# A fused attention and feed-forward kernel: group 0's second product by seven block products, w_out cast by its load, one block product added in PSUM

## The chip, the cores and the metric

The kernel runs on one core of a Trainium2 chip. The time is device microseconds of one execution, and two kernels are compared by it. The core has five engines that the text names as the profile does: PE (the matrix engine; PEld is its loading of weights, which runs beside the matmuls), DVE, ACT, POOL (GpSimd) and SP, whose queue issues most DMAs. All DMAs run on the core's 16 DMA engines.

## The reference

```python
def phi(x, c, s):                       # c, s: cosine and sine of the position
    r = np.maximum(x, 0.0)
    return np.concatenate([r * c, r * s], axis=-1)
q_p, k_p = phi(q, cos_w, sin_w), phi(k, cos_w, sin_w)
kv = np.einsum('bhsf,bhsd->bhfd', k_p, v)
z = np.sum(k_p, axis=2)
num = np.einsum('bhsf,bhfd->bhsd', q_p, kv)
den = np.einsum('bhsf,bhf->bhs', q_p, z)[..., None] + 1e-06
x = (num / den).transpose(0, 2, 1, 3).reshape(B * S, H * D)
h = x @ w_in
out = np.maximum(0.01 * h, h) @ w_out
```

Eight batches of 576 tokens with eight heads of 64 give 4608 rows of 512; `w_in` is 512 x 2048 and `w_out` 2048 x 512. Inputs and output are float32.

## The kernel before

The rows are worked off in nine groups of 512. Groups 0 to 7 are the first 512 tokens of a batch each, group 8 holds the last 64 tokens of all eight. For a group, q is masked and scaled into fp16 (`q_part`), as is k (`k_part`), and v is cast (`v_main`, with `v_tail` or `v_mask` for the last 64 tokens). PE then makes kv of the batch (`kv_sums` in two halves for batches 0 and 1, `kv_all`, line 290, later), and numerator and denominator (`num`, line 381). DVE divides (line 397), and the result is transposed to `xT` by PE or by a DMA.

Group 0's first product runs as 128x512 matmuls (line 496), 16 column tiles m of `w_in` with four chunks each, and its second product too: `ffn2_mm` (line 629) adds 16 matmuls for each of four row tiles tt into a PSUM bank `ps_o`, 64 in all. Group 1's first product is plain as well. From group 2's first product and group 1's second on, each product is cut into 2x2 blocks and made by seven block products in place of eight (Winograd's form): `p1` (line 745) for the first product, `p2` (line 846) for the second, each matmul 128x256, with sums of blocks made by DVE (`x_sums`, `w1_sums`, `g_sums`, `w2_sums`). Some blocks of later groups are cut once more (`p4th`, line 963, 128x128).

One unit of `p1` covers four column tiles and has four PSUM banks: two that units take in turn (here called a), `SEED` and `JOIN`. Product 1 goes into a, and ACT copies it to `SEED` (`seed`, line 755), where product 2 is added and ACT takes the leaky ReLU of the sum (block 11, `lrelu`, line 758). Product 6 is added in a, copied by ACT to SBUF (`u_copy`, line 765); product 7 is added in a and copied too; product 4 is added, and ACT makes block 21. Product 5 goes into `JOIN`. DVE adds it to the second copy (`u_add`, line 252), product 3 is added in `JOIN`, DVE adds that to the first copy, and one activation over both copies makes blocks 12 and 22 (`u_lrelu`, line 772).

Loads are issued on SP's queue, in the order q, k and v of batch 0, `w_in` (eight DMAs of 512 KB), two of the four MB of `w_out`, q of batch 1, the third MB, halves of k and v of batch 1, the fourth MB, and so on. `w_in` and `w_out` come as float32 into staging tiles; POOL, DVE and ACT cast them into the fp16 tiles (`cast_w1`, `cast_w2`, line 249). The order of everything is written out by hand: each step is given a position, the table `PLACE` overrides positions, `OTHER` names steps that change between DVE and ACT, and the steps are issued in order of their positions. Each engine runs its part strictly in that order.

```python
    for _, _, f, args in sorted(line, key=lambda e: e[:2]):
        f(*args)
```

Of the kernel before, what the change touches and what calls it, by code (L numbers as in the profile page):

```python
# [18 lines left out]
def kernel(  # L19
# [429 lines left out]


# [172 lines left out]

    def ffn2_mm(g, i):
        tt, part = divmod(i, 4)
        if part == 0 and ("ps_o", g, tt) not in st:
            st["ps_o", g, tt] = psum("o", [P, DM], dt.float32, "ps_o")
        for m in range(4 * part, 4 * part + 4):
            nc.tensor.matmul(  # L629
                st["ps_o", g, tt],  # L630
                lhsT=st["g", g][:, m, tt * P : (tt + 1) * P],
                rhs=w2[:, m, :],
                start=(m == 0),
                stop=(m == NFT - 1),
            )
# [1167 lines left out]
```

## Time and profile before

| | us |
|---|---|
| median of three runs | 268.2 (266.79 to 268.61) |
| the profiled execution | 267.86 |
| its span, first to last instruction | 266.1 |
| first matmul of any kind, on blanks | 1.09 |
| group 0's first product has PE to itself from | 18.90 |
| group 0's second product begins | 31.01 |

The span is 1.8 us shorter than the execution's own time. Two views carry the reading: the table of windows, which gives each engine's busy time and the DMA engines' share in a stretch, and the chain of waits, which lists in order of time what the end was waiting for. A row of the timeline names in brackets how long the engine stood idle before it and what ended that.

### The profile page before, as it was taken

To read this page: it belongs to the slowest core of one execution; us is meant where nothing else is said; L and a number is where in the kernel's file an instruction comes from. 1 tells how busy PE (TensorE), PEld (TensorE's weight loads), DVE (VectorE), ACT (ScalarE), POOL (GpSimd) and SP (SyncE) were. 2 spreads that over 40 slices of the span, in tenths; PEclk is the share of its full clock that TensorE was granted. 3 is DMA by queue.
4 is the path that set the end of the run, shared out by engine and by line. 5 is a ranking of instruction groups with operands and counts; after the bars stand their busy time and mean duration, and the time that the engine had idled before them with its cause. 6 is when DMAs were issued, how large, how long until landed. Compare 5 with 4: busy or idle time off the path is not lost.

```text
span 266.1 us, 7209 instructions
## 1 busy us (share of the span) xinstructions
PE 260.3 (98%) x2874; PEld 229.7 (86%) x2874; DVE 233.5 (88%) x550; ACT 217.6 (82%) x400; POOL 9.9 (4%) x21
## 2 busy tenths in 40 slices
PE   8999999999999999999999999999999999999994
PEld 6885466765999889999999999999999999999994
DVE  5882799997998899999989899999999988996993
ACT  8756567876999999999889889999988877878751
POOL 1056001000000000000000000000000000000000
PEclk9999999999999999999999999999999999999999
DMA  6999999999999999998997899957645043300216
GB/s 222 357 395 410 401 388 370 370 213 303 273 242 145 278 312 210 332 146 264 265 229 181 248 288 235 141 200 170 92 101 197 22 80 60 121 1 4 98 65 155
DMA packets 87153, 57.09 MB, mean 215 GB/s; under 512 B 56656, under 2 KB 82256, under 8 KB 86608
## 3 DMA queue, kind: packets, MB, share of 16 engines
q1 hardware_dynamic: 86672, 56.24, 81.4%
q8 instruction: 22, 0.36, 0.6%
q10 hardware_dynamic: 448, 0.39, 0.5%
q14 instruction: 11, 0.09, 0.1%
HBM read 36.70 MB, written 9.44 MB: 173 GB/s over the span
## 4 chain that ended last, share of the span: by engine, by line
PE 89%; DMA 4%; DVE 2%; SPq 2%; ACT 1%; issue 0%; ACTq 0%
PE ps_h L745 30%; PE ps_o L846 24%; PE ps_h L496 10%; PE ps_o L963 8%; PE ps_o L629 5%; PE ps_num L381 3%; PE ps_kv L290 2%; DMA xT<-xs 2%; DMA vtl<-in_v_dram 2%; PE ps_h L846 2%; PE ps_h L963 1%; PE ps_numh L581 1%; PE ps_kvh L290 1%; SPq L93 1%; SPq L103 1%; DVE u L252 1%
## 5 line engine op out<-in xcount | busy, mean ns | idle before, releaser
L745 PE MATMUL ps_h<-xT,w 128*128 128x256 f16 x336 | 49.2, 273 | 0.2 <-DMA xT<-xs 0.2
L745 PEld LDWEIGHTS <-w 128*128 128x128 f16 x448 | 47.3, 113 | 1.0 <-issue 0.4
L846 PEld LDWEIGHTS <-g 128*128 128x128 f16 x408 | 38.7, 98 | 3.6
L252 DVE TENSOR_TENSOR u<-ps_h,u 128x512 f32<-128x512 f32 x56 | 38.4, 685 | 3.8 <-PE ps_h L745 2.5
L745 PEld LDWEIGHTS <-wa 128*128 128x128 f16 x336 | 35.9, 113 | 1.3 <-issue 1.0
L765 ACT COPY u<-ps_h 128x512 f32<-128x512 f32 x56 | 32.9, 592 | 4.3 <-PE ps_h L745 3.6
L758 ACT ACTIVATE g<-ps_h 128x512 f16<-128x512 f32 x56 | 33.8, 605 | 2.5 <-PE ps_h L745 2.3
L745 PE MATMUL ps_h<-xw,wa 128*128 128x256 f16 x224 | 33.6, 272 | 0.5 <-DVE u L252 0.3
L772 ACT ACTIVATE g<-u 128x1024 f16<-128x1024 f32 x28 | 29.7, 1065 | 2.3 <-DVE u L252 2.2
L496 PE MATMUL ps_h<-xT,w 128*128 128x512 f16 (+1 forms) x152 | 29.6, 345 | 0.0
L846 PEld LDWEIGHTS <-gs 128*128 128x128 f16 x256 | 24.4, 98 | 2.3
L846 PE MATMUL ps_o<-w,g 128*128 128x256 f16 x192 | 25.9, 273 | 0.0
L846 PE MATMUL ps_o<-wb,g 128*128 128x256 f16 x184 | 25.6, 272 | 0.0
L496 PEld LDWEIGHTS <-w 128*128 128x128 f16 x152 | 16.3, 113 | 9.0
L864 ACT COPY ob<-ps_o 128x512 f32<-128x512 f32 (+1 forms) x32 | 18.1, 566 | 2.9 <-PE ps_o L846 1.8
L397 DVE TENSOR_TENSOR xs<-ps_num,rden 128x512 f16<-128x512 f32 x28 | 19.4, 691 | 1.0
L846 PE MATMUL ps_o<-w,gs 128*128 128x256 f16 x120 | 17.0, 273 | 0.0
L755 ACT COPY ps_h<-ps_h 128x512 f32<-128x512 f32 x28 | 16.4, 584 | 0.7 <-PE ps_h L745 0.2
L745 PE MATMUL ps_h<-xT,wa 128*128 128x256 f16 x112 | 16.8, 273 | 0.0
L745 PE MATMUL ps_h<-xw,w 128*128 128x256 f16 x112 | 16.8, 273 | 0.0
L846 PE MATMUL ps_o<-wb,gs 128*128 128x256 f16 x120 | 15.9, 272 | 0.0
L629 PE MATMUL ps_o<-w,g 128*128 128x512 f16 x64 | 15.3, 379 | 0.0
(148 smaller groups left out, 502.0 us busy)
## 6 DMA issues: line engine op xcount, KB each, us to landing
qst<-in_q_dram SPq DMA_DIRECT2D x7, 1024.0 KB, 7.3
out_dram<-ob SPq DMA_DIRECT2D x14, 512.0 KB, 3.0
kst<-in_k_dram SPq DMA_DIRECT2D x6, 1024.0 KB, 8.6
vst<-in_v_dram SPq DMA_DIRECT2D x6, 1024.0 KB, 7.7
w1st<-in_moe_w_in_dram SPq DMA_DIRECT2D x8, 512.0 KB, 9.0
w2st<-in_moe_w_out_dram SPq DMA_DIRECT2D x4, 1024.0 KB, 12.4
kst<-in_k_dram SPq DMA_DIRECT2D x4, 512.0 KB, 7.1
vst<-in_v_dram SPq DMA_DIRECT2D x4, 512.0 KB, 6.4
```

The lines of the kernel that those rows point to most:

```text
L252: nc.vector.tensor_tensor(out=o, in0=a, in1=b, op=ALU.add)
L397: nc.vector.tensor_tensor(out=xs, in0=ps[:, :, 0 : 4 * NE].rearrange("p a (b e) -> p a b e", e=NE)[:, :, :, 0:D], in1=rden.rearrange("p (a ...
L496: nc.tensor.matmul(ps[:, lo:hi], lhsT=w1[m // 4][c // 2][:, c % 2, m % 4 : 512 : 4], rhs=st["xT", g][:, c, lo:hi], start=(c == 0 and lo == 0),
L629: nc.tensor.matmul(st["ps_o", g, tt], lhsT=st["g", g][:, m, tt * P : (tt + 1) * P], rhs=w2[:, m, :], start=(m == 0), stop=(m == NFT - 1),)
L745: nc.tensor.matmul(bank[:, p], lhsT=w(c), rhs=st["xb", g][n][:, c], start=(fresh and p == 0 and c == 0), stop=(c == 1), skip_group_check=True,
L755: nc.scalar.copy(bank1[bj], bank1[bi])
L758: nc.scalar.activation(st["g" + nm, g][:, 2 * t : 2 * t + 2], bank1[bi], AF.Lrelu)
L765: nc.scalar.copy(st["u", g, t][:, n], bank1[bi])
L772: nc.scalar.activation(st["gt", g][:, :, 1, 2 * t : 2 * t + 2], st["u", g, t], AF.Lrelu)
L846: nc.tensor.matmul(bank[..., lo:hi], lhsT=st[G2[n], g][:, m, pair * P : (pair + 1) * P], rhs=W2[n](m)[:, lo:hi], start=(fresh and m == 0), ...
L864: nc.scalar.copy(o_at(g, half_, col, pair), bank_of(bi, pair, pair is None))
L963: nc.tensor.matmul(quad_at(g, bi, *QUAD[i]), lhsT=lhsT, rhs=rhs, start=(m == 0 and (i == 2 or (i == 4 and g == NG - 1))), stop=(m == 3), s ...
```

## The change

Six things change.

1. Group 0's second product is made by seven block products: `ffn2_mm` goes, and `p2` is called for group 0 with 16 matmuls for each product. DVE makes the four sums of blocks of group 0's activations in halves (`g_sums`), all sums of `w_out` blocks are needed earlier (`w2_sums`), and the output leaves by four ACT copies, three DVE adds and two stores of 512 KB where it was four copies and four stores of 256 KB. A third PSUM bank (`third_bank`) holds products 5 and 3.
2. `load_w2` is issued by POOL straight into the fp16 tile `w2`, so that the DMA casts. `cast_w2` and its staging tiles go.
3. In a unit of `p1`, product 5 is copied to SBUF by ACT (`p5_copy`), DVE adds it to bank a and writes the sum into `SEED` (after products 1 and 6) and, after product 7, into `JOIN` (`p5_add`); product 3 is added in `SEED` by PE. Blocks 12 and 22 are then activated each from its bank. `u_copy`, `u_add`, `u_lrelu` go.
4. Group 1's first product, as plain as before, is issued in halves of a column tile (`f1_unit`).
5. Pools with several buffers take them in a fixed turn (`Turns`); the staging tiles by a list (`STAGE`).
6. `PLACE` and `OTHER` are other tables: nearly every step has another position, and `OTHER` names 96 steps, most of them maskings of q and k, where it named 25.

```diff
+    class Turns:
+        def tile(self, shape, dtype, name, tag=None, bufs=None):
+            tag, bufs = tag or name, bufs or self.bufs
+            n = self.count[tag] = self.count.get(tag, -1) + 1
+            n = self.order[n] if self.order else n % bufs
+            return self.places.tile(shape, dtype, name=name, tag=f"{tag}__{n}", bufs=1)
...
     def load_w2(i):
-        t = staged([P, 4, DM], "w2st", i > 1)
-        nc.sync.dma_start(t, w2v[i])
-        st["w2", i] = t
+        nc.gpsimd.dma_start(w2[:, 4 * i : 4 * i + 4, :], w2v[i])
...
-    def u_copy(g, t, n, bi):
-        if n == 0:
-            st["u", g, t] = tpool.tile([P, 2, 2, N2], dt.float32, name="u", tag="u")
-        nc.scalar.copy(st["u", g, t][:, n], bank1[bi])
-
-    def u_add(g, t, n, bi):
-        u = st["u", g, t][:, n]
-        add(u, bank1[bi], u)
+    def p5_copy(g, t, bi):
+        st["p5", g, t] = tpool.tile([P, 2, N2], dt.float32, name="p5", tag="p5")
+        nc.scalar.copy(st["p5", g, t], bank1[bi])
+
+    def p5_add(g, t, bi, to):
+        add(bank1[to], bank1[bi], st["p5", g, t])
...
+            banks = {2: SEED, 3: SEED, 5: JOIN}
...
+                (1, seed, (t, a, SEED)), (2, lrelu, ("11", t, SEED)),
+                (5, p5_copy, (t, JOIN)), (5.01, p5_add, (t, a, SEED)),
+                (7, p5_add, (t, a, JOIN)), (3, lrelu_12, (t, SEED)),
+                (7.01, lrelu_22, (t, JOIN)), (4, lrelu, ("21", t, a)),
...
+    def first_p2(n, bi, fresh):
+        for u in range(2):
+            for pair in range(2):
+                now(p2, 0, n, pair, u, bi, fresh and u == 0 and pair == 0)
...
         "first_loads": {
-            (0,): -940.5, (1,): -893.5, (10,): -869.33, (12,): -861.25
+            (0,): -999.8, (3,): -987.43, (2,): -876.5, (4,): -874.0, (1,): -856.83, (5,): -846.6,
```

How the change moves instructions is seen in three places. The first is POOL's queue at the program's start, up to the last step that POOL does at all; `vmain` is the cast v, `w_0_0` to `w_3_1` are the eight fp16 tiles of `w_in`. Before:

```order
L249 CAST vmain<-vst 128x8x64 x2
L249 CAST w_0_0_102<-w1st 128x512 x2
L249 CAST w_0_1_103<-w1st 128x512 x2
L249 CAST w_2_0_106<-w1st 128x1024
L249 CAST w_2_1_107<-w1st 128x1024
L249 CAST w_3_1_109<-w1st 128x1024
L249 CAST w_3_0_108<-w1st 128x1024
L249 CAST vmain<-vst 128x16x64
```

The same place now, where `w_113` is the fp16 tile of `w_out`:

```order
L162 DMA w_113<-in_moe_w_out_dram 128x2048
L266 CAST vmain<-vst 128x8x64 x2
L266 CAST w_0_0_105<-w1st 128x512
L162 DMA w_113<-in_moe_w_out_dram 128x2048
L266 CAST w_0_0_105<-w1st 128x512
L266 CAST w_0_1_106<-w1st 128x512 x2
L266 CAST w_2_1_110<-w1st 128x1024
L266 CAST w_2_0_109<-w1st 128x1024
L266 CAST w_3_0_111<-w1st 128x1024
L266 CAST w_3_1_112<-w1st 128x1024
L162 DMA w_113<-in_moe_w_out_dram 128x2048 x2
```

The first MB of `w_out` (its rows for m 0 to 3) now stands ahead of everything that POOL waits for, the third MB (m 8 to 11) between two casts of `w_in`, and the second and fourth behind the last of them.

The second place is DVE while PE does the end of group 0's first product. Before, with `w_110` the fp16 tile of `w_out`, `wa` sums of `w_in` blocks:

```order
L252 TENSOR_TENSOR wa_0_211<-w_2_0_106,w_2_1_107 128x1024
L255 TENSOR_TENSOR wa_0_213<-wa_0_211,w_0_0_102 128x1024
L249 CAST w_110<-w2st 128x2048
L252 TENSOR_TENSOR wa_1_212<-w_3_0_108,w_3_1_109 128x256x2
L255 TENSOR_TENSOR wa_1_214<-wa_1_212,w_1_0_104 128x256x2
L249 CAST w_110<-w2st 128x2048
L255 TENSOR_TENSOR wa_1_216<-w_1_1_105,wa_1_214 128x256x2
L241 TENSOR_SCALAR qp<-qst,cos_t 128x8x64
```

Now, with `gs` and `g` sums of group 0's activation blocks and `wb` sums of `w_out` blocks:

```order
L269 TENSOR_TENSOR wa_0_214<-w_2_0_109,w_2_1_110 128x1024
L272 TENSOR_TENSOR gs_518<-g 128x1024
L272 TENSOR_TENSOR wa_0_216<-wa_0_214,w_0_0_105 128x1024
L272 TENSOR_TENSOR gs_518<-g 128x1024
L272 TENSOR_TENSOR wb_220<-w_113 128x1024
L272 TENSOR_TENSOR w_113<-w_113 128x4x256
L272 TENSOR_TENSOR wb_221<-w_113,wb_220 128x1024
L272 TENSOR_TENSOR gs_519<-g,gs_518 128x1024
L269 TENSOR_TENSOR g<-g 128x4x256
L272 TENSOR_TENSOR wb_222<-w_113,wb_221 128x1024
```

The casts of `w_out` are gone, and the sums that the block products need stand in their place.

The third place is ACT in group 2's first product. Before, `ps_h_1221` and `ps_h_1222` are the banks a, `ps_h_1223` is `SEED` (`JOIN`, `ps_h_1224`, is read by DVE alone):

```order
L765 COPY u<-ps_h_1222 128x512
L755 COPY ps_h_1223<-ps_h_1221 128x512
L772 ACTIVATE g<-u 128x2x512
L758 ACTIVATE g<-ps_h_1222 128x512
L247 CAST vmain<-vst 128x16x64
L758 ACTIVATE g<-ps_h_1223 128x512
L765 COPY u<-ps_h_1221 128x512
```

Now `ps_h_1289` and `ps_h_1290` are the banks a, `ps_h_1291` is `SEED` and `ps_h_1292` is `JOIN`:

```order
L765 COPY p_1487<-ps_h_1292 128x512
L239 ACTIVATE vtail<-vtl,odd 128x4x64 x2
L759 ACTIVATE g<-ps_h_1289 128x512
L857 COPY ob<-ps_o_539 128x2x256
L264 CAST vmain<-vst 128x16x64
L759 ACTIVATE g<-ps_h_1291 128x512
L756 COPY ps_h_1291<-ps_h_1289 128x512
L759 ACTIVATE g<-ps_h_1292 128x512
```

The last activation that reads `SEED` in one unit now stands right ahead of the copy that fills `SEED` for the next; before, `SEED` was free after block 11, early in its unit.

More of the change, by code (lines that the diff above doesn't have):

```diff
@@ L60 @@
     const = pool("const", 1)
-    stage = pool("stage", 3)
+    stage = pool("stage", 3, order=STAGE)
     kvtail = pool("kvtail", 3)
@@ L68 @@
     xtpool = pool("xT", 2)
+    xwpool = pool("xw", 2)
+    opool = pool("out", 2)
     early = pool("early", 4, stack=first)
@@ L559, in kv_sums @@
     def kv_sums(b, hg, where, blanks=0):
-        ps = psum(where, [P, MAIN], dt.float32, "ps_kvh")
+        if where is None:
+            ps = st["third"][:, 1]
+        else:
+            ps = psum(where, [P, MAIN], dt.float32, "ps_kvh")
         idle(blanks, ps)
@@ L855, in o_tiles @@
     def o_tiles(g):
-        for half_ in range(2):
+        for half_ in (g % 2, 1 - g % 2):
             st["ob", g, half_] = opool.tile([P, 2, DM], dt.float32, name="ob", tag="ob")
@@ L1593 @@
         if m == 12:
-            now(cast_w2, 0, DVE)
             now(first_loads, 11)
@@ L1599 @@
         if m == 14:
-            now(cast_w2, 1, DVE)
             now(first_loads, 12)
@@ L1604 @@
             now(ffn1_out, 0, m - 1)
+            if m == 7:
+                for u in range(2):
+                    now(g_sums, 0, 3, 4 * u, 4 * u + 4)
+            if m in (11, 15):
+                for n in (1, 2):
+                    now(g_sums, 0, n, m - 11, m - 7)
     for j in range(J):
@@ L1608 @@
             now(q_part, 1, j, part, DVE)
-    now(cast_w2, 2, DVE)
     now(kp_tiles, 1)
@@ L1639 @@
         now(k_part, 1, j, 1, DVE, 4, 8)
-    for jp in range(2):
-        now(num_mm, 1, jp, 0, "h")
-        now(num_div, 1, jp, 0)
-    now(v_main, 1, 4, 8, POOL)
-    now(ffn2_mm, 0, 4 * 2 + 3)
-    now(ffn2_mm, 0, 4 * 3 + 3)
-    for tt in (2, 3):
-        now(ffn2_copy, 0, tt, ACT)
-        now(ffn2_store, 0, tt)
-    now(ffn2_mm, 0, 4 * 0 + 3)
+    now(num_mm, 1, 0, 0, "h")
+    now(num_div, 1, 0, 0)
+    now(v_main, 1, 4, 8, ACT)
+    first_p2(7, 0, False)
+    now(o_add, 0, 1, 1, 0)
+    now(num_mm, 1, 1, 0, "h")
+    now(num_div, 1, 1, 0)
+    now(kv_sums, 1, 1, None)
+    now(kv_copy, 1, 1, ACT)
     for jp in range(2):
@@ L1673 @@
         put(n - 1000, f, *args)
-    put(-1, quarters, 1)
-    order = [m + up for m in range(0, NH, 2) for up in (0, 1, NH, NH + 1)]
-    for n, m in enumerate(order):
-        put(2 * n, f1_pair, 1, m)
-    put(31, open_banks)
-    put(35, blank_seed)
+    put(1.1 * 7 * 4 - 0.06, open_banks)
+    put(1.1 * 7 * 4 - 0.05, blank_seed)
+    put(1.1 * 7 * 4, w1_sums, 0, 3, 0, 4)
+    for lo in (0, 2):
+        put(1.1 * 7 * 4, w1_sums, 1, 3, lo, lo + 2)
+    for at_, f, args in f1_stream(1):
+        put(1.1 * at_, f, *args)
     for g in range(2, NG):
```

382 lines of the change are left out of this document (177 added, 205 removed), and 455 rows, old and new, of tables (OTHER, PLACE).

## The prediction

> **What bounds the kernel now.** I read the page's busy shares first, with the shares of the chain of waits by engine, and then the table of windows (length, busy time and count of PE, PEld, DVE, ACT, POOL; granted PE clock; share of the DMA engines; GB/s).
>
> ```profile
> PE 260.3 (98%) x2874; PEld 229.7 (86%) x2874; DVE 233.5 (88%) x550; ACT 217.6 (82%) x400; POOL 9.9 (4%) x21
> PE 89%; DMA 4%; DVE 2%; SPq 2%; ACT 1%; issue 0%; ACTq 0%
> ...
> 5.00:6.00 1.00, 1.00 (x8) 0.77 (x7) 1.00 (x5) 1.00 (x4) 0.00 (x0) 1.00 0.94 278
> 10.00:11.00 1.00, 1.00 (x12) 0.90 (x10) 1.00 (x5) 0.89 (x3) 0.00 (x0) 1.00 1.10 382
> ...
> 25.00:31.00 6.00, 6.00 (x29) 3.13 (x28) 3.55 (x5) 3.29 (x4) 1.38 (x2) 1.00 1.03 406
> 31.00:37.00 6.00, 6.00 (x43) 3.23 (x41) 5.12 (x13) 2.73 (x3) 0.00 (x0) 1.00 1.09 386
> 37.00:43.00 6.00, 6.00 (x57) 3.52 (x56) 5.96 (x16) 4.99 (x8) 0.00 (x0) 1.00 1.05 380
> 43.00:50.00 7.00, 7.00 (x85) 4.51 (x84) 6.46 (x19) 4.77 (x10) 1.16 (x1) 1.00 1.10 375
> 50.00:56.00 6.00, 6.00 (x41) 4.05 (x39) 6.00 (x16) 5.76 (x9) 0.00 (x0) 1.00 1.14 282
> 82.00:90.00 8.00, 7.95 (x91) 7.51 (x90) 7.28 (x18) 7.97 (x14) 0.00 (x0) 1.00 0.98 264
> 90.00:100.00 10.00, 9.49 (x98) 8.70 (x96) 9.04 (x23) 9.57 (x20) 0.00 (x0) 1.00 1.22 267
> 100.00:130.00 30.00, 30.00 (x370) 28.82 (x369) 28.61 (x64) 28.07 (x52) 0.00 (x0) 1.00 1.10 231
> 220.00:250.00 30.00, 29.88 (x316) 28.58 (x315) 26.19 (x55) 23.09 (x48) 0.00 (x0) 1.00 0.13 46
> ```
>
> PE is the bound: it is full in nearly every window at clock 1.00, and the idle time in the rows that have any is 0.05, 0.51 and 0.12, together 0.68 us. So the time is the moment at which dense work starts, plus PE's work, plus waits. The DMA share of about 1 to beyond 50 us is the second fact: what is put ahead in the transfers there moves what stands behind. The third is DVE, with 23.54 of the 25 us from 31 to 56. The start is seen in the chain (start, length, piece) and in the timelines of POOL, DVE and SP.
>
> ```profile
> 18.90 12.11 PE ps_h L496 x64
> 31.01 2.59 PE ps_o L629 x12
> 68.00 2.62 PE ps_o L846 x24
> ...
> 13.40 1.17 POOL L249 CAST vmain<-vst 128x512 f16<-128x512 f32 x2 [11.53 <-DMA vst<-in_v_dram]
> 14.89 1.18 POOL L249 CAST w<-w1st 128x512 f16<-128x512 f32 x2 [0.32 <-DMA w1st<-in_moe_w_in_dram]
> 21.68 1.04 POOL L249 CAST w<-w1st 128x1024 f16<-128x1024 f32 x1 [0.30 <-DMA w1st<-in_moe_w_in_dram]
> 24.35 2.03 POOL L249 CAST w<-w1st 128x1024 f16<-128x1024 f32 x2 [1.63 <-DMA w1st<-in_moe_w_in_dram]
> ...
> 7.67 1.36 DVE L249 COPY qpT<-ps_qt 128x1024 f16<-128x1024 f16 x2 [0.37 <-PE ps_qt L366]
> 12.00 0.35 DVE L241 TENSOR_SCALAR kpm<-kst,cos_t 128x256 f16<-128x256 f32 x1 [0.54 <-DMA kst<-in_k_dram]
> 26.83 1.23 DVE L249 CAST w<-w2st 128x2048 f16<-128x2048 f32 x1 [2.66 <-DMA w2st<-in_moe_w_out_dram]
> 29.28 1.23 DVE L249 CAST w<-w2st 128x2048 f16<-128x2048 f32 x1 [0.42 <-DMA w2st<-in_moe_w_out_dram]
> ```
>
> The brackets show that POOL's casts of v and of `w_in` wait for their transfers: the transfers set the start. Two MB of `w_out` came in one after the other, and their casts waited for them at 26.83 and 29.28: 2.45 us for 1 MB.
>
> **The change part by part.** *Seven block products in group 0.* PE loses 64 matmuls of 2.59/12 = 0.216 us, 13.8 us, and gains 7 x 16 = 112 of 2.62/24 = 0.109 us, 12.2 us: -1.6 us, on the path since PE is dense there. Bounds: -1.6, and -1.2 if each of the 112 goes at the pace of its weight load (113 ns below).
>
> *The sums for it.* DVE gains eight sums of activations at 0.68 us and three output adds at 0.685 us, 7.5 us, and loses three casts of `w_out` at 1.224 us and one of 0.693 us, 4.4 us; ACT loses a cast of 1.047 us. Sums of `w_out` blocks are only made earlier.
>
> ```profile
> L745 PEld LDWEIGHTS <-w 128*128 128x128 f16 x448 | 47.3, 113 | 1.0 <-issue 0.4
> L252 DVE TENSOR_TENSOR u<-ps_h,u 128x512 f32<-128x512 f32 x56 | 38.4, 685 | 3.8 <-PE ps_h L745 2.5 <-PE ps_o L963 0.6 <-ACT u L765 0.4
> L255 DVE TENSOR_TENSOR gs<-g 128x1024 f16<-128x1024 f16 x16 | 10.9, 682 | 1.5 <-PE ps_o L846 1.4
> L249 DVE CAST w<-w2st 128x2048 f16<-128x2048 f32 x3 | 3.7, 1224 | 3.1 <-DMA w2st<-in_moe_w_out_dram 3.1
> L249 DVE CAST w<-w2st 128x1024 f16<-128x1024 f32 x1 | 0.7, 693 | 0.0
> L247 ACT CAST w<-w2st 128x1024 f16<-128x1024 f32 x1 | 1.0, 1047 | 0.0
> L758 ACT ACTIVATE g<-ps_h 128x512 f16<-128x512 f32 x56 | 33.8, 605 | 2.5 <-PE ps_h L745 2.3
> L765 ACT COPY u<-ps_h 128x512 f32<-128x512 f32 x56 | 32.9, 592 | 4.3 <-PE ps_h L745 3.6
> L772 ACT ACTIVATE g<-u 128x1024 f16<-128x1024 f32 x28 | 29.7, 1065 | 2.3 <-DVE u L252 2.2
> L755 ACT COPY ps_h<-ps_h 128x512 f32<-128x512 f32 x28 | 16.4, 584 | 0.7 <-PE ps_h L745 0.2
> L864 ACT COPY ob<-ps_o 128x512 f32<-128x512 f32 x28 | 16.6, 594 | 2.0 <-PE ps_o L846 0.9 <-DVE ps_o L252 0.6
> L252 DVE TENSOR_TENSOR ps_o<-ps_o,x 128x512 f32<-128x512 f32 x6 | 4.2, 694 | 0.0
> ```
>
> From 31 to 56 DVE has 25 - 23.5 = 1.5 us free for a net 3.1 us, and ACT (2.73 + 4.99 + 4.77 + 5.76 = 18.25 of 25) has 6.7 us free, besides 1.0 us from the lost cast. The table `OTHER` can move maskings to ACT, so I cost this at 0; without that cover it is 3.1 - 1.5 = +1.6 us, the upper bound.
>
> *Product 5 added in PSUM.* Of the 28 units each cost ACT 584 + 2 x 592 + 2 x 605 + 1065 = 4043 ns and now costs 584 + 592 + 4 x 605 = 3596 ns, 12.5 us less in all; DVE's 56 additions go from 685 to 694 ns, +0.5 us. PE makes the same matmuls. Beside a dense PE both are worth 0; what DVE's adds hold up if late is products 7 and 3, which have to wait for them where they waited for ACT's copies and DVE before. The wait at `SEED` is the last rival.
>
> *`w_out` by POOL.* The first MB is issued ahead of all that POOL waits for, where before it came behind all of `w_in`; the third is issued between the first casts of `w_in`. Where the DMA engines are full, 1 MB ahead delays q, k, v and `w_in` by up to 2.45 us; no row shows a casting load, so the ends are 0 (it fills shares left open, as the 0.94 at 5 us) and 2.45. It writes half the bytes of a plain load, and half of 2.45 is 1.2; between that and the whole I take 1.8 for each. Of the first MB's 1.8, DVE's 0.37 and 0.54 us of idle before 13 us can be taken back by the new split of maskings; I take half, 0.4. That leaves +1.4 for the start. The third MB delays the later tiles of `w_in`. PE needs that for m 8 at 31.01 - 8 x 4 x 0.216 = 24.1, and POOL had it at 21.68 + 1.04 = 22.7: 1.4 us of slack, so 1.8 - 1.4 = +0.4 (ends 0 and 1.05). The second and fourth MB go out behind POOL's last cast, at 24.35 + 2.03 + 1.8 = 28.2. The new order uses the second behind the four column tiles m 12 to 15 (3.46 us, begun at 27.55 + 1.8), six quarters of block products (2.62) and two transposes (0.9), at about 36.3. One MB on half the engines, 4.9 us, has landed by 33.1. Cost 0.
>
> The Trainium skill, "DMA: Bandwidth & Descriptors", section "Queues, rings and completion order", says that each DMA engine takes turns between the queues it has work for, a packet at a time. By it the early MB would have its full share at once, so the whole 2.45 and 1.05 count, 3.5 in place of my two terms' 1.8: 269.8. No run here shows two queues loading at once.
>
> *Group 1's halves, the fixed turns, the positions.* The plain matmuls of group 1 are as many and as long as before, 0. The fixed turns can gain or lose a wait for a buffer; the rows with idle time hold 0.68 us, so 0.68 is the most to be gained. Half of it goes, since the 0.51 is a wait for a transposing DMA, which stays: -0.3.
>
> Sum: -1.6 + 1.4 + 0.4 - 0.3 = -0.1 on the profiled execution's 267.86 (span 266.1 and 1.8 around it), 267.8. It stands 0.3 under the median of the runs, 268.2, so 268.1 is compared with the median. Its own range, from half a price per MB (1.2 - 0.4, and 0 for the third: a sum of -1.1) to the full one with nothing taken back (2.45 + 1.05: +1.6): 267.1 to 269.8.
>
> **The rivals.** *Faster.* The casting loads fit beside the others, and the start comes earlier by DVE's 0.91 us of idle: -1.6 - 0.9 - 0.68 = -3.2, so 265.0. For it: the share of 0.94, and halved writes. Against it: the 1.10 at 10 us, where `w_in` comes in. It needs a start no later than 18.90.
>
> *Slower, by late descriptors.* POOL's loads do not start while DVE is packed with work. The stretch to look at is DVE's long run without a gap, whose first and last rows are:
>
> ```profile
> 31.88 0.49 DVE L241 TENSOR_SCALAR qp<-qst,cos_t 128x512 f16<-128x512 f32 x1 [1.04 <-DMA qst<-in_q_dram]
> ...
> 39.08 0.35 DVE L224 TENSOR_SCALAR vtail<-vtl,odd 128x256 f16<-128x256 f32 x1
> ```
>
> If the second MB, issued at 28.2, is held up to the end of such a run at 39.4, it lands at 41.9 and PE waits 41.9 - 36.3 = 5.6 us: 273.7. It decides from 2.8 us of waiting on (270.9), and half-way between is 272.3. For it: DVE's idle time before 26.83 and 29.28, which left gaps, was waiting for the old staged loads. Against it: 3.7 us from 28.2 to 31.88 suffice for an MB that is not hindered. The Trainium skill, "SBUF — State Buffer", section "SBUF: two separate sides", names this trap: a load issued by GpSimd has its descriptors written by GpSimd, which is locked out of a shared port while DVE runs an operation that uses both ports. No run here shows such a load.
>
> *Slower, by `SEED`.* It is now read last by the activation of block 12, 605 ns, right ahead of the copy that fills it for the next unit, 584 ns: 1.19 us from product 3 to the next unit's product 2. In 6 of 27 passages the new order puts only 12 matmuls (1.31 us) or hardly more between. If ACT has a 594-ns output copy ahead, 0.47 us is missing each time; in 6 it is 2.8 us: 270.9, and with a few of the longer passages 271.5. Against it: ACT is 1.9 of 30 us free at 100 us, and has 0.45 us less per unit now.
>
> *The sums are not hidden:* +1.6 from above, 269.7, still within 1%.
>
> **How the numbers follow.** About 1%, 2.7 us, is what a measurement of this kernel can tell from no change: under 265.5 is faster, over 270.9 slower. My forecast 0.58, the faster rival 0.17, unhidden sums 0.06, late descriptors 0.11, `SEED` 0.08. So faster 0.17, same 0.58 + 0.06 = 0.64, slower 0.19. The range leaves out the two slower rivals (0.19) and reaches down to the faster one: 264.8 to 270.9.
>
> **What would show it.** In the profile after: the dense stage begins 1.4 us later than 18.90, with POOL's first casts of v and `w_in` as much behind 13.40 and 14.89; the stretch of group 0's second product takes 12.2 us of PE's time; ACT has some 13 us less; DVE stays above 23 of 25 us from 31 to 56. It is wrong if PE waits for a POOL load or on ACT ahead of a product 2, or if the dense start does not move.

## The result, and the profile after

| | before | after |
|---|---|---|
| median of the runs, us | 267.61 (266.79 to 268.61) | 277.15 (275.65 to 277.78) |
| profiled execution | 267.86 | 277.58 |
| its span | 266.1 | 275.8 |

The ratio is 1.0347, with a 95% interval of 1.0285 to 1.0408: slower by 3.5%, and 6 us above the range that was forecast. (One run of the later version e13, 282.29 us at a lower clock, is left out of its median and its ratio.) The busy times and the shares of the chain of waits by engine, on the page of the changed kernel:

```profile
PE 261.7 (95%) x2914; PEld 234.0 (85%) x2914; DVE 235.3 (85%) x541; ACT 212.0 (77%) x416; POOL 11.8 (4%) x24
PE 74%; DMA 7%; DVE 5%; SPq 5%; ACT 5%; issue 2%; POOL 1%; ACTq 0%; DVEq 0%
```

PE is busy about as long as before, but its share of the chain fell from 89% to 74%, and DMA, SP's queue, DVE and ACT have 22% of it where they had 9%. The table of windows of the changed kernel (same columns as in the prediction) says where:

```profile
11.00:19.00 8.00, 4.50 (x68) 4.03 (x66) 6.18 (x18) 6.44 (x14) 2.50 (x5) 0.79 1.06 349
19.00:25.00 6.00, 4.54 (x63) 3.88 (x61) 3.21 (x10) 3.57 (x6) 1.62 (x3) 1.00 1.06 317
25.00:31.00 6.00, 4.94 (x29) 2.87 (x26) 0.69 (x1) 3.75 (x4) 1.87 (x2) 1.00 1.05 375
31.00:37.00 6.00, 5.79 (x27) 3.09 (x28) 5.77 (x7) 2.67 (x4) 4.03 (x5) 1.00 0.87 258
37.00:43.00 6.00, 5.36 (x52) 4.11 (x50) 5.96 (x13) 5.41 (x9) 0.00 (x0) 1.00 1.05 234
43.00:50.00 7.00, 6.79 (x94) 5.87 (x93) 6.53 (x19) 5.73 (x12) 0.00 (x0) 1.00 1.09 384
50.00:57.00 7.00, 7.00 (x95) 6.38 (x93) 6.64 (x17) 6.86 (x13) 0.00 (x0) 1.00 0.66 210
```

PE idles 3.5 us from 11 to 19, 1.5 and 1.1 us in the next two windows, and DVE, which was to be packed from 31 on, works 0.69 of 6 us from 25 to 31. The same matmul can be looked up in both traces, and the difference of its start times tells how late the changed kernel is at that place:

| start of | before | after | later by |
|---|---|---|---|
| m 4, the first 128x512 matmul | 20.49 | 26.57 | 6.1 |
| m 8 | 23.94 | 31.21 | 7.3 |
| m 12 | 27.39 | 34.70 | 7.3 |
| the last matmul | 262.31 | 271.16 | 8.9 |
| (end of the span) | 266.1 | 275.8 | 9.7 |

So three quarters of the loss are made before PE reaches m 8. What follows was added up from the start times of PE's matmuls: for each shape, the time from one start to the next beyond the median of that shape, here called lost time. Between m 12 and group 1's first product the seven products win their 1.6, and 1.65 of lost time takes it back, where before has none. Past 57 us the changed kernel has 1.5 more of lost time than before (4.1 against 2.6), and the stretch behind the last matmul is 0.9 longer. PE's timeline of the changed kernel (start, length, what, count, idle time before and what ended it):

```profile
14.83 1.04 PE L307 MATMUL ps_kvh<-vmain,kpm 128*128 128x65 f16 x16 [3.50 <-ACT vmain L264]
24.31 2.02 PE L515 MATMUL ps_h<-xT,w 128*128 128x256 f16 x17 [0.84 <-ACT xT L264]
31.21 6.24 PE L515 MATMUL ps_h<-xT,w 128*128 128x512 f16 x28 [1.03 <-POOL w L266]
41.15 0.62 PE L383 MATMUL ps_qt<-ident,qp 128*128 128x128 f16 x8 [0.65 <-DVE qp L258]
```

and POOL's, which casts what comes in:

```profile
1.81 0.70 POOL L162 DMA_DIRECT2D w<-in_moe_w_out_dram  x1
16.38 1.23 POOL L266 CAST vmain<-vst 128x512 f16<-128x512 f32 x2 [13.87 <-DMA vst<-in_v_dram]
18.29 0.54 POOL L162 DMA_DIRECT2D w<-in_moe_w_out_dram  x1
29.13 2.03 POOL L266 CAST w<-w1st 128x1024 f16<-128x1024 f32 x2 [6.36 <-DMA w1st<-in_moe_w_in_dram]
31.36 2.86 POOL L266 CAST w<-w1st 128x1024 f16<-128x1024 f32 x2 [0.21 <-DMA w1st<-in_moe_w_in_dram]
34.17 1.06 POOL L162 DMA_DIRECT2D w<-in_moe_w_out_dram  x2
```

The cast of v comes 3.0 us later than the 13.40 of before, the last two casts of `w_in` 7.0 later than 24.35; each waits for its transfer. On ACT, too, a cast of `w_in` waits, and the copies of `xT` that PE waits for at 24.31 stand behind it:

```profile
22.73 1.05 ACT L264 CAST w<-w1st 128x1024 f16<-128x1024 f32 x1 [1.12 <-DMA w1st<-in_moe_w_in_dram]
```

What took the transfers' time stands in the view of the DMA queues. First from 2 to 12 us, then from 17 to 33 us, in the changed kernel (packets, MB, share of 16 engines in the window; q1 is SP's queue, q0 POOL's):

```profile
q1 hardware_dynamic: 3041, 2.36, 73.2%
q0 software_dynamic: 144, 0.52, 27.0%
```

```profile
q1 hardware_dynamic: 3508, 4.79, 87.3%
q0 software_dynamic: 144, 0.52, 16.2%
```

27.0% of 10 us and 16.2% of 16 us are 2.7 and 2.6 us of all engines for one MB read and cast to half as much: not the half price, and taken at once.

The DVE timeline of the changed kernel shows why DVE could not use its idle time:

```profile
31.19 0.69 DVE L269 TENSOR_TENSOR wa<-w,w 128x1024 f16<-128x1024 f16 x1 [5.04 <-POOL w L266]
31.80 1.52 DVE L272 TENSOR_TENSOR gs<-g 128x1024 f16<-128x1024 f16 x1
```

The sums of group 0's activations stand behind a sum of `w_in` blocks that waits for POOL's cast, so the late tile holds them as well.

### The profile page after: what moved, and what is told of

It reads as the page before. It is cut to its first block, busy times and chain, and to the rows that moved or that the text cites. A ratio compares the mean times of both kernels' runs of the same rounds, so it can differ in the third digit from the quotient of the medians.

```text
span 275.8 us, 7308 instructions
## 1 busy us (share of the span) xinstructions
PE 261.7 (95%) x2914; PEld 234.0 (85%) x2914; DVE 235.3 (85%) x541; ACT 212.0 (77%) x416; POOL 11.8 (4%) x24
## 4 chain that ended last, share of the span: by engine, by line
PE 74%; DMA 7%; DVE 5%; SPq 5%; ACT 5%; issue 2%; POOL 1%; ACTq 0%; DVEq 0%
PE ps_h L746 29%; PE ps_o L839 24%; PE ps_o L956 7%; DMA w1st<-in_moe_w_in_dram 5%; PE ps_h L515 4%; PE ps_num L398 2%; SPq L122 2%; DMA vtl<-in_v_dram 2%; PE ps_kv L307 2%; SPq L112 2%; PE ps_h L839 2%; PE ps_h L956 1%; SPq L159 1%; ACT g L727 1%; DVE wb L272 1%
## 5 line engine op out<-in xcount | busy, mean ns | idle before, releaser
L759 ACT ACTIVATE g<-ps_h 128x512 f16<-128x512 f32 x112 | 65.2, 601 | 16.7 <-PE ps_h L746 11.7
L839 PEld LDWEIGHTS <-g 128*128 128x128 f16 x488 | 45.9, 98 | 5.2 <-DVE g L269 0.3
L269 DVE TENSOR_TENSOR ps_h<-ps_h,p 128x512 f32<-128x512 f32 x56 | 39.0, 697 | 7.3 <-ACT p L765 2.9
L746 PE MATMUL ps_h<-xw,wa 128*128 128x256 f16 x224 | 32.1, 272 | 0.0
L839 PE MATMUL ps_o<-w,g 128*128 128x256 f16 x224 | 30.6, 272 | 0.0
L839 PEld LDWEIGHTS <-gs 128*128 128x128 f16 x288 | 27.5, 98 | 2.8
L839 PE MATMUL ps_o<-wb,g 128*128 128x256 f16 x200 | 27.5, 272 | 0.0
L857 ACT COPY ob<-ps_o 128x512 f32<-128x512 f32 (+1 forms) x35 | 19.9, 568 | 6.3 <-PE ps_o L839 4.6
L269 DVE TENSOR_TENSOR ob<-ps_o,ob 128x512 f32<-128x512 f32 (+1 forms) x24 | 16.2, 674 | 1.7 <-PE ps_o L839 1.0
L765 ACT COPY p<-ps_h 128x512 f32<-128x512 f32 x28 | 16.6, 591 | 1.0 <-PE ps_h L746 0.8
L956 PEld LDWEIGHTS <-g 128*128 128x128 f16 x208 | 14.2, 98 | 0.4
```

Source lines behind the costliest of these rows:

```text
L269: nc.vector.tensor_tensor(out=o, in0=a, in1=b, op=ALU.add)
L746: nc.tensor.matmul(bank[:, p], lhsT=w(c), rhs=st["xb", g][n][:, c], start=(fresh and p == 0 and c == 0), stop=(c == 1), skip_group_check=True,
L759: nc.scalar.activation(st["g" + nm, g][:, 2 * t : 2 * t + 2], bank1[bi], AF.Lrelu)
L765: nc.scalar.copy(st["p5", g, t], bank1[bi])
L839: nc.tensor.matmul(bank[..., lo:hi], lhsT=st[G2[n], g][:, m, pair * P : (pair + 1) * P], rhs=W2[n](m)[:, lo:hi], start=(fresh and m == 0), ...
L857: nc.scalar.copy(o_at(g, half_, col, pair), bank_of(bi, pair, pair is None))
```

## The experiments

My first theory after the result was that the early loads alone do it. The rival was that DVE, with more to do from 31 to 56, is a bound of its own that the late start hides.

### The early loads: one MB, two MB, cast or not

Before's kernel, with the first MB alone loaded by POOL ahead of everything; once cast by the load (e4), once as float32 into a staging tile of its own, cast by DVE as before (e5, where `t` is that tile and the load goes to it).

```diff
-        t = staged([P, 4, DM], "w2st", i > 1)
-        nc.sync.dma_start(t, w2v[i])
+        if i == 0:
+            t = None
+            nc.gpsimd.dma_start(w2[:, 4 * i : 4 * i + 4, :], w2v[i])
+        else:
+            t = staged([P, 4, DM], "w2st", i > 1)
+            nc.sync.dma_start(t, w2v[i])
...
-            (0,): -940.5, (1,): -893.5,
+            (0,): -999.8, (1,): -893.5,
```

> The kernel before with only the first MB of w_out loaded by POOL, first of all, with the cast in the load; the other three as before. Theory A (what stands ahead in the transfers delays what stands behind): dense work starts 2.5 to 3.5 us late, and DVE has one cast of 1.22 us less: 269 to 271. A load that hides beside the others would give 266 to 268.

> As the run beside it, but POOL's early MB is loaded as float32 into a staging tile and cast by DVE as before. Theory A: the same delay of 2.5 us at the start as with the cast, and DVE's cast stays: 270 to 272. Rival C (it is the cast in the load that slows the transfers): a start less than 1 us late and 267 to 268.5.

Measured: 270.68 us against 267.98 (ratio 1.0101, 1.0072 to 1.0131) and 271.05 (1.0119, 1.0077 to 1.0162). POOL's timeline of the kernel with the casting load:

```profile
15.88 1.16 POOL L253 CAST vmain<-vst 128x512 f16<-128x512 f32 x2 [13.38 <-DMA vst<-in_v_dram]
17.23 1.17 POOL L253 CAST w<-w1st 128x512 f16<-128x512 f32 x2 [0.19 <-DMA w1st<-in_moe_w_in_dram]
24.65 1.04 POOL L253 CAST w<-w1st 128x1024 f16<-128x1024 f32 x1 [0.31 <-DMA w1st<-in_moe_w_in_dram]
```

and of the one with the plain load:

```profile
15.53 1.17 POOL L254 CAST vmain<-vst 128x512 f16<-128x512 f32 x2 [13.02 <-DMA vst<-in_v_dram]
24.95 1.04 POOL L254 CAST w<-w1st 128x1024 f16<-128x1024 f32 x1 [0.31 <-DMA w1st<-in_moe_w_in_dram]
```

The casts, at 13.40, 14.89 and 21.68 in before, come 2.5, 2.3 and 3.0 us later with the casting load; with the plain one the first and the last of them come 2.1 and 3.3 later. The median time is 2.7 and 3.1 us longer. So 1 MB ahead delays what stands behind it by 2.1 to 3.3 us, whether it is cast on its way or not. In the two profiled executions, which are among the shortest of their kernels (269.43 and 270.00), 1.1 us of it comes back past 57 us, where lost time falls from before's 2.6 to 1.5 us. The Trainium skill, "DMA: Bandwidth & Descriptors", section "Queues, rings and completion order", has each engine take turns between the queues it has work for; the traces agree in so far as POOL's queue was served at once beside SP's, with 27.0% and 73.2% of the engines' time from 2 to 12 us in the changed kernel.

Then before with all of `w_out` loaded by POOL at the changed kernel's places, its own casts taken out (e2).

```diff
-        t = staged([P, 4, DM], "w2st", i > 1)
-        nc.sync.dma_start(t, w2v[i])
-        st["w2", i] = t
+        nc.gpsimd.dma_start(w2[:, 4 * i : 4 * i + 4, :], w2v[i])
...
-        copy(eng, w2[:, 4 * i + lo : 4 * i + hi, :], st["w2", i][:, lo:hi])
+        pass
...
-            (0,): -940.5, (1,): -893.5,
+            (0,): -999.8, (1,): -942.5,
```

> The kernel before with one part of the change alone: w_out is loaded by POOL with the cast in the load, the first MB first of all, the second between the first two casts of w_in, the others behind the last; DVE and ACT cast nothing of it. Theory A: dense work starts some 3 us later, m 8 about 7 us later, the time is 273 to 276. Rival B: 267 to 269.

Measured: 272.81 against 267.39 (1.0183, 1.0127 to 1.0238). m 4 starts at 25.67 where before has 20.49, 5.2 us later. This is not yet the second of the early MB: POOL issues that one at 19.19, and the second half of kv, at 19.04 where before has 14.12, is 4.9 late by then, in e4 only 2.5 (16.60). What e2 has besides, and e4 has not, is a lower clock behind PE's wait of 2.76 us for v at 11.8:

```profile
11.00:19.00 8.00, 4.77 (x50) 3.81 (x49) 4.86 (x17) 3.90 (x9) 1.53 (x3) 0.69 1.00 317
```

The second early MB is seen further on: POOL's last casts of `w_in` come 7.1 us late (31.41 after 24.35), and PE's timeline has m 12 at

```profile
33.49 3.64 PE L494 MATMUL ps_h<-xT,w 128*128 128x512 f16 x16 [0.70 <-POOL w L247]
```

6.1 us behind before's 27.39, and the last matmul is still 5.1 late, though DVE was relieved of all casts of `w_out`. The loads alone are worth 5.4 us in before, the lower clock that follows the wait included.

A last look at the loads moved half of them back (e10): before, with only the third and fourth MB by POOL, behind its last cast of `w_in`.

```diff
+        if i > 1:
+            nc.gpsimd.dma_start(w2[:, 4 * i : 4 * i + 4, :], w2v[i])
+            return
-        t = staged([P, 4, DM], "w2st", i > 1)
+        t = staged([P, 4, DM], "w2st", False)
```

> The kernel before with the third and fourth MB of w_out loaded with the cast by POOL behind its last cast of w_in; the first two by SP and cast by DVE as before. DVE loses 1.22 + 0.69 us and ACT 1.05 us of work between 35 and 42 us. Theory D (DVE's work there stands on the path, one for one): 265.5 to 266.8, if the two MB land by 40 us. If DVE's work is off the path: 267 to 268; if the casting loads come late or delay q, k and v of batch 1 by more than that: 269 to 271.

Measured: 274.41 against 267.98 (1.0239, 1.0208 to 1.027). Now q of batch 1 is what they pass. DVE's and PE's timelines of this kernel:

```profile
38.38 0.48 DVE L244 TENSOR_SCALAR qp<-qst,cos_t 128x512 f16<-128x512 f32 x1 [6.12 <-DMA qst<-in_q_dram]
```

```profile
29.65 1.89 PE L499 MATMUL ps_h<-xT,w 128*128 128x512 f16 x8
39.32 1.04 PE L369 MATMUL ps_qt<-ident,qp 128*128 128x128 f16 x8 [5.19 <-DVE qp L244]
40.15 3.62 PE L633 MATMUL ps_o<-w,g 128*128 128x512 f16 x8
```

DVE had q at 31.88 before. There is no slack behind the start either; and from 36.9 to 43.8 us, in and behind its wait of 5.19 us, PE has half the clock, so that eight 128x512 matmuls take 3.62 us and not 1.89.

### The loads undone in the changed kernel

`w_out` comes by SP again, as float32 into staging tiles and behind `w_in`, and DVE casts it (e1).

```diff
     def load_w2(i):
-        nc.gpsimd.dma_start(w2[:, 4 * i : 4 * i + 4, :], w2v[i])
+        st["w2", i] = staged([P, 4, DM], "w2st", i % 2 == 1)
+        nc.sync.dma_start(st["w2", i], w2v[i])
+
+    def cast_w2(i, eng):
+        copy(eng, w2[:, 4 * i : 4 * i + 4, :], st["w2", i])
...
+        "cast_w2": {
+            (2,): -857.0, (0,): -856.9, (1,): -839.0, (3,): -795.0
...
-            (0,): -999.8, (3,): -987.43,
+            (3,): -909.0, (0,): -908.9,
```

> The changed kernel with one part undone: w_out is loaded by SP as float32 behind w_in (MB 3 and 1 ahead of q of batch 1) and cast by DVE. Theory A (the two MB that POOL loads ahead of v and w_in cost the time, the rest of the change is worth about what its terms say): column tile m 8 of group 0 begins at about 24 us as before, not at 31, and the time is 267 to 270. Rival B (the new order and product 5's new path cost it, the loads only move waits): 273 or more, with waits of PE on ACT or DVE behind 40 us.

Measured: 276.81 against 267.39 (1.0352, 1.0301 to 1.0404): nothing gained. m 4 is back at 22.41 and m 12 at 29.32, 4.2 and 5.4 us earlier than in the changed kernel (22.41 is still 1.9 behind before; before's order of the start wins back 0.8 of it in e8), and group 1's first product starts at 56.01, only 1.0 earlier. Windows of this kernel, and PE's timeline in them:

```profile
31.00:37.00 6.00, 4.19 (x33) 2.72 (x31) 5.93 (x12) 4.68 (x7) 0.00 (x0) 1.00 1.08 392
37.00:43.00 6.00, 4.11 (x45) 3.53 (x44) 5.97 (x14) 3.25 (x7) 0.00 (x0) 1.00 1.05 378
```

```profile
35.18 1.05 PE L843 MATMUL ps_c<-wb,g 128*128 128x256 f16 x8 [1.81 <-DVE g L273]
37.77 0.62 PE L387 MATMUL ps_qt<-ident,qp 128*128 128x128 f16 x8 [0.66 <-DVE qp L262]
40.50 1.03 PE L843 MATMUL ps_o<-w,g 128*128 128x256 f16 x8 [1.23 <-DVE w L270]
```

DVE is full, and PE, which had every microsecond of 31 to 43 in before, waits for it 3.7 of 12. The time lies in the range of rival B, but not for its reason: up to 57 us this kernel has 8.0 us more of lost time than before, past it 1.6 more. The same loads by POOL, but issued behind the casts of `w_in` where the first two tiles are no more held up (e3), end in the same place:

```diff
-            (0,): -999.8, (3,): -987.43,
+            (3,): -909.2, (0,): -909.1,
```

> The changed kernel with the first and third MB of w_out issued by POOL behind its casts of w_in's third quarter instead of at the start and between the first casts. Theory A: m 8 begins at about 24 us; the loads then delay only w_in's last quarter and the first block products, 269 to 273. Rival C (a load with a cast slows the other transfers more than its bytes, wherever it stands): 274 to 277. Rival B: 276 to 278.

Measured: 279.15 against 267.39 (1.0429, 1.0382 to 1.0476). PE's timeline has one long wait for a sum of DVE, and DVE's timeline has the wait for `w_out` that it stands behind; POOL had issued that load at 24.03:

```profile
37.58 1.89 PE L839 MATMUL ps_c<-wb,g 128*128 128x256 f16 x8 [4.47 <-DVE g L269]
```

```profile
34.30 0.69 DVE L272 TENSOR_TENSOR wb<-w 128x1024 f16<-128x1024 f16 x1 [5.26 <-DMA w<-in_moe_w_out_dram]
```

### What DVE's work costs by itself

Before, with eight more sums on DVE between 31 and 48 us, as long as group 0's; their results go nowhere (e9).

```diff
+    def more(n):
+        if n == 0:
+            st["more"] = morepool.tile([P, 4, N2], dt.float16, name="more")
+        t = st["g", 0]
+        sub(st["more"], t[:, 4:8, 0:N2], t[:, 4:8, N2:MAIN])
+
+    for n, pos in enumerate((-829.1, -826.1, -823.1, -820.1, -815.1, -805.1, -800.1, -790.1)):
+        put(pos, more, n)
```

> The kernel before with eight more operations on DVE between 31 and 48 us, each like a sum of group 0's activation blocks (128x1024 fp16, 0.68 us); their result is not used. Theory D: DVE has 1.5 us free from 31 to 56 us for 5.5 us, so the time goes up by 2.5 to 4.5 us, to 270 to 272. Rival (DVE's work there is off the path, as the prediction took it): 267 to 268.5.

Measured: 272.66 against 267.43 (1.0194, 1.0134 to 1.0253). 8 x 0.68 = 5.4 us of DVE cost 5.2 us of time. A window, with the lower clock (0.76) that follows PE's wait, and the wait itself:

```profile
43.00:50.00 7.00, 4.49 (x21) 1.92 (x20) 6.97 (x12) 2.44 (x6) 1.37 (x1) 0.76 1.10 373
```

```profile
46.77 2.72 PE L630 MATMUL ps_o<-w,g 128*128 128x512 f16 x6 [2.51 <-DVE w L250]
```

So DVE is the second bound of this stretch in before. But PE, back from its wait at 46.77, had half the clock until 49.84; that is worth up to 1.5 of the 5.2 us (an estimate: half of 3.07), so it stays open whether DVE's 1.5 us of free time were a reserve that was used up first. The other way round, the sums of group 0's activations are left out of the changed kernel, with the loads undone (e7) and with the loads as they are (e13; the same edit on the changed kernel).

```diff
     def g_sums(g, n, lo=0, hi=NH):
+        if g == 0:
+            return
...
-                lhsT=st[G2[n], g][:, m, pair * P : (pair + 1) * P],
+                lhsT=st[(G0 if g == 0 else G2)[n], g][:, m, pair * P : (pair + 1) * P],
```

> The first experiment's kernel without group 0's eight sums of activation blocks (products 6 and 7 and the summed blocks read unsummed ones, so group 0's output is another): DVE has 5.5 us less from 26 to 50 us, PE the same matmuls. Theory D: PE's waits on DVE there nearly vanish, 272 to 274. Rival B: 275 to 277.

> The changed kernel with POOL's casting loads where the change has them, and only group 0's eight sums of activation blocks left out (group 0's output is another). Theory of two bounds: the late w_in still sets column tiles m 4 to 15, only the 1.3 us of PE's waits from 40 to 47 us go: 275.5 to 276.8. If DVE's work alone were the cause: 271 to 273.

Measured: 275.75 against 267.43 (1.0313, 1.0256 to 1.0369), 1.1 under e1, and 277.68 against 268.19 (1.0308, 1.0222 to 1.0394), nothing under the changed kernel. With the loads in place the sums cost nothing more, since the loads bind; with the loads undone the casts of `w_out` are back on DVE.

Taking both away (e14): e7, with no values of `w_out` cast at all and its tile set to zero by DVE from 20 to 24 us, where it idles.

```diff
     def cast_w2(i, eng):
-        copy(eng, w2[:, 4 * i : 4 * i + 4, :], st["w2", i])
+        nc.vector.memset(w2[:, 4 * i : 4 * i + 4, :], 0.0)
...
-            (2,): -857.0, (0,): -856.9, (1,): -839.0, (3,): -795.0
+            (2,): -901.0, (0,): -900.9, (1,): -900.8, (3,): -900.7
```

> As the kernel with neither cost, but w_out's fp16 tile is set to zero from 20 to 24 us, where DVE waits for POOL, in place of the setting at the start, which took DVE 8 us there. w_out is loaded but not cast, group 0's eight sums are left out; all outputs are others. Theory of two bounds: m 4 begins at 22.4 us as in the first experiment, PE's waits on DVE from 31 to 50 us (4.7 us there) are under 1.5, 270 to 273. A third cause on PE's path between 25 and 57 us would leave 275 or more.

Measured: 273.19 against 267.88 (1.0189, 1.0142 to 1.0235), 4.0 us under the changed kernel. Its windows, and the longest waits of PE (for what; us in total, times, longest):

```profile
31.00:37.00 6.00, 6.00 (x54) 4.42 (x52) 3.39 (x7) 4.85 (x8) 0.00 (x0) 1.00 1.08 394
37.00:43.00 6.00, 5.61 (x75) 4.75 (x73) 4.38 (x13) 5.26 (x9) 0.00 (x0) 1.00 1.05 377
```

```profile
PE ps_h L750 <- DVE ps_h L273: 1.4, 1, 1.4
PE ps_h L519 <- ACT xT L268: 1.3, 1, 1.3
```

PE is full again from 31 to 37. This is what shows the two bounds: the loads undone alone give 0.3 us (e1), the sums left out alone nothing (e13), both together 4.0, of which 1.4 come already with the casts still on DVE (e7). The changed kernel without early loads and with neither more nor less work on DVE than it has was not run, so how the 4.0 divide between the sums and the casts that come back with SP's loads stays open. An earlier try of the same (e12), with the tile set to other values at the program's start, tells nothing: the four settings took DVE 1.76 us each there, and m 4 came at 27.92, 5.2 behind e14's; 278.51 against 268.19 (1.0357, 1.0281 to 1.0434).

> The changed kernel with both suspected costs taken away: w_out is loaded by SP as float32 behind w_in as in the first experiment, but not cast (the fp16 tile is set to constants once at the start, before q comes), and group 0's eight sums of activation blocks are left out; outputs of all groups are others. Theory of two bounds (late w_in by the early loads, and DVE from 25 to 50 us; either alone gives nearly the whole loss): PE's waits on DVE from 31 to 50 us fall from 4.7 us to under 1.5 and the time to 270 to 272, what is left over 267.6 being the later start (about 2) and waits past 80 us (about 2). If a third cause holds the time: 275 or more.

Could POOL do the casts (e6: e1 with the casts there)?

```diff
-        put(0, cast_w2, i, DVE)
+        put(0, cast_w2, i, POOL)
```

> The first experiment's kernel (w_out loaded by SP as float32), with its four casts on POOL instead of DVE. Theory D (with the data there in time, DVE is what group 0's block products wait for: it was full from 31 to 56 us before, and now has eight sums of activations and four sums of w_out blocks more there): DVE gets 4.9 us free from 28 to 47 us and the waits of PE on it, 4.7 us there, go down to about 1: 272 to 274. Rival B (the new order past 57 us costs most): 275 to 277.

Measured: 277.67 against 267.43 (1.0373, 1.0328 to 1.0419): no gain, though DVE lost 4.9 us of casts. POOL's and DVE's timelines, side by side, show two reasons:

```profile
35.74 2.06 POOL L270 CAST w<-w2st 128x2048 f16<-128x2048 f32 x1 [3.55 <-DMA w2st<-in_moe_w_out_dram]
```

```profile
32.22 0.69 DVE L276 TENSOR_TENSOR wb<-w 128x1024 f16<-128x1024 f16 x1 [1.79 <-POOL w L270]
35.36 0.68 DVE L276 TENSOR_TENSOR wb<-w,wb 128x1024 f16<-128x1024 f16 x1
35.97 2.11 DVE L273 TENSOR_TENSOR wa<-w,w 128x512 f16<-128x512 f16 x1
```

DVE waits for POOL's casts, and it is slowed beside them: at 35.97 half the elements of the row above take three times as long, and the sum lasts as long as POOL's cast. A third is seen on PE, which waits for a sum of DVE and then has half the clock:

```profile
35.50 1.36 PE L843 MATMUL ps_c<-wb,g 128*128 128x256 f16 x8 [2.25 <-DVE g L273]
```

```profile
37.00:43.00 6.00, 4.79 (x31) 3.51 (x30) 5.96 (x10) 1.82 (x3) 2.23 (x2) 0.51 1.05 376
```

### What is left: the start's order, the clock, and the dense stage

e8 is e1 with the steps up to m 4 in before's order and on before's engines; e17 is the same start in e14, with e15's edit besides.

```diff
+    START = (
+        ('q_part', (0, 0, 0, 0, 4), 'DVE'),
...
+        ('ffn_banks', (), ''),
+    )
+    for n, (name, key, eng) in enumerate(START):
...
+                line[i] = (-1000 + 0.5 * n, at_, f, tuple(e if any(a is x for x in (DVE, ACT, POOL)) else a for a in args))
```

> The first experiment's kernel with the order and the engines of the start (all steps ahead of column tile m 4 of group 0) as in the kernel before. Theory D: m 4 begins at 20.5 us in place of 22.4 and POOL's casts of w_in come without the wait for the later tile first, so DVE starts on its sums 2 us earlier; 273 to 276, since DVE stays the bound. If the start alone set the end: 274.9, exactly as much earlier as m 4 is. Rival B: 275 to 277.

> Neither bound (e14: no sums of group 0's activations, no casts and no values of `w_out`, w2 zero; casts of v batch 4 later as in e16), and the start in before's order and on before's engines. Theory (the start's new order is a third, smaller bound, hidden so far behind the two others): the first 128x512 matmul comes at about 20.5 to 21.5 instead of 22.4, PE's wait of 0.9 to 1.5 us at 19 to 20 us goes, and the time falls by 1 to 2 us from 272.85 to 271 to 272. Rival (the start is not what is left; the rest lies in the new order past 57 us): m 4 comes earlier but the time stays within 0.5 us of 272.85. Second rival: the third tile of w_in lands when it lands, and m 4 stays at 22.4.

Measured: 277.58 against 267.43 (1.0365, 1.0319 to 1.041) and 273.24 against 267.7 (1.0208, 1.017 to 1.0246). m 4 comes 0.8 us earlier in e8 (21.58) and 1.2 earlier than e14's 22.76 in e17 (21.55), and nothing of it is left at the end: in e8 PE waits 3.3 us for one sum of DVE and has half the clock from then to 41.5 us, in e17 new waits between 33 and 41 us and from 76 us on take it. For e17 the theory and the second rival fall, and the first rival holds.

The idle time of 3.5 us at 11 in the changed kernel is followed by a lower clock (0.79 in its window). e11 fills it with 34 more blank matmuls.

```diff
-    now(kv_sums, 0, 0, "t", 14)
+    now(kv_sums, 0, 0, "t", 31)
```

> The changed kernel with 34 more matmuls on blanks ahead of the first sums of kv, 3.7 us that fill PE's wait for v at 11 to 15 us. If the lower granted clock at 11 to 19 us (0.79) stands on the path: 276 to 276.5, 0.7 to 1.2 us less. If DVE's lateness takes it up again further on: 276.8 to 277.6 as before.

Measured: 278.97 against 267.98 (1.0407, 1.0354 to 1.0461). The clock stays at 1.00, and nothing is won: m 4 starts at 26.55 beside 26.57, since what PE waits for there comes when it comes.

Elsewhere the clock does count. In e2, e3, e6, e8, e9 and e10 the clock falls to one half in or right behind a wait of PE of 2.25 to 5.19 us, and stays there for 3.4 us (e9) or 6.8 us (the others); in e1, e4, e7 and e14 it is 1.00 until the last matmuls. A full PE loses half of such a stretch, as far as it lies behind the wait: an estimate of up to 1.5 us in e9 and up to 2.8 in e8 (35.87 to 41.52). So the times of those six are not the price of the edit alone.

In the dense stage, DVE's additions for product 5 stand behind a cast of v of batch 4 that waits for its transfer. The DVE timeline of e14 (the changed kernel has the same at 85.76, with 0.61 us of waiting):

```profile
81.80 0.69 DVE L270 CAST vmain<-vst 128x1024 f16<-128x1024 f32 x1 [1.93 <-DMA vst<-in_v_dram]
82.40 0.69 DVE L273 TENSOR_TENSOR ps_h<-ps_h,p 128x512 f32<-128x512 f32 x1
```

e15 moves these casts behind the additions in the changed kernel, e16 in e14.

```diff
-            (4, 0): 65.29, (4, 2): 67.408, (4, 1): 69.57,
+            (4, 0): 69.74, (4, 2): 75.1, (4, 1): 75.11,
```

> The changed kernel with three steps moved: the casts of v of batch 4 on DVE and ACT, which stood ahead of product 5's additions in the second unit of group 2's first product and there waited for v's load, stand behind them. Theory E (product 5's additions make DVE and ACT links of each unit, so a step ahead of them that waits for a load stops PE at 86 to 92 us): PE's 0.8 us of waits there go, 0.3 to 1.0 us less than the changed kernel's 277.15. Rival (these waits are taken up by others behind): no change.

> Both runs beside it together: neither early loads nor DVE's sums and casts of w_out, and v's casts of batch 4 behind product 5's additions (outputs are others, as in the first of the three). If the three causes are all that there is: 268.5 to 271, the rest over 267.6 being the start (2 us later at m 4) less product 2's saving of 1.6 us.

Measured: 276.80 (1.0343, 1.0299 to 1.0387) and 272.85 (1.0189, 1.0155 to 1.0223), both 0.35 us under the kernel they are made from, which the intervals don't tell from nothing; a wait of 1.16 us turns up further on (it ends at 92.63 and 89.66), at product 3, which waits for an addition of product 5.

What is left of e17, 5 us of span over before, adds up so: up to 57 us it holds 3.1 us more of lost time than before, past 57 us 2.9 more; the seven products give back 1.6, and the stretch behind the last matmul is 0.8 longer. That the new order of the dense stage costs these 2.9 is the likely reading, since e14 (2.9), e16 (2.2) and e17 (2.9) all show them; the order was not tried apart from the rest of the change, nor was product 5's new path, so it stays open which of the two does it. The times of e3, e6, e8, e10, e11, e13 and e16 lie in none of the ranges that were given for them, those of e2, e9 and e14 up to 0.7 us outside the theory's; in e1 and e7 the range of rival B was hit. e16 says that the three causes named there are not all that there is. The two bounds account for 4.0 of the 9.5 us, the rest is open in its parts. None of the versions beats the kernel before.

## Why the prediction was wrong

- *Seven block products, -1.6 us:* borne out. The 112 matmuls have 109 ns from start to start (median), as the rest.
- *The early loads, +1.4 and +0.4:* the step that failed first. The mechanism was right, and the prediction named it; "between that and the whole I take 1.8 for each" was the wrong size, since writing half the bytes saves nothing (2.6 and 2.7 us of engine time, 2.7 us of time in e4), and nothing of the 0.4 is seen to come back at the start. The third MB was charged against the slack of m 8 alone, 1.4 us, though it also goes out ahead of the tiles for m 4 to 7: ACT's cast of one waits 1.12 us for its transfer at 22.73, and the `xT` copies that PE waits for stand behind it. Beside e1, which has the same start without the early loads, the changed kernel is 4.2 late at m 4 (26.57 against 22.41) and 5.3 at m 8 (31.21 against 22.41 + 16 x 0.216 = 25.87), in place of 1.4 and 1.8.
- *The Trainium skill's rule of turns between queues,* weighed there at 269.8, came nearer: the load did have its share at once and cost its whole time. Its 3.5 us still fell short of the 5.3 at m 8, as it kept the slack of 1.4 for the third MB; without that slack it would have been 2 x 2.45 = 4.9.
- *"The table `OTHER` can move maskings to ACT, so I cost this at 0":* the second step that failed. Maskings did move: ACT's busy time fell by 5.6 us and not by some 13. But DVE has 24.9 us of 26 in 31 to 57 all the same, since "sums of `w_out` blocks are only made earlier" is four more sums of 0.68 us in just this stretch (eight from 31 to 56, where before has four). What such work costs beside a full PE shows in e9: 5.2 us for 5.4, the lower clock behind the wait included, and not 0. The upper bound of +1.6 was a subtraction of busy times where a due time was needed.
- *Two costs in one place:* the sum added terms, but these are two bounds on one stretch, and undoing either leaves the other (e1 -0.3, e13 nothing, e14 -4.0 us).
- *Product 5 in PSUM, 0,* and *the fixed turns and positions, -0.3:* the sign of the second is wrong. m 4 is 1.9 us late in e1 without any early load, 1.5 us more are lost past 57 us, and 0.9 behind the last matmul. Some of the 1.5 lies on the path that I had costed at 0: products 7 and 3 "have to wait for them", as the prediction said, and from 82 to 100 us the changed kernel loses 1.7 us where before loses 1.1. Moving the cast of v that stands in front won nothing clear of noise (e15), so what makes the rest is not shown.
- *The rivals:* late descriptors did not come. POOL issued its last two loads at 34.17 in 1.06 us with DVE packed from 31.19 on, and nothing waited for them. `SEED` did not come either: of PE's waits on ACT ahead of a first product's matmul, the changed kernel's view of waits has only these:

```profile
PE ps_h L746 <- ACT g L759: 0.5, 1, 0.5
PE ps_h L746 <- ACT ps_h L756: 0.3, 1, 0.3
```

What the rivals lacked was a DVE that becomes the bound with a price of its own beyond +1.6.
- *What would show it:* the start moved by 6.1 and not 1.4; POOL's first casts by 3.0 and 2.8 (17.73 after 14.89); "DVE stays above 23 of 25" is the one sign that was seen, and it was the sign of the second bound.
